# A Fourier transform and MLP kernel on one Trainium2 core: a fourth output buffer, a new place for the broadcast rows, and earlier transforms

## The chip, the cores and the metric

The kernel runs on one core of a Trainium2 chip. The metric is the device time in microseconds (us) of one execution; of several executions the median is given.

The names used below are those of the profile: PE is the engine of matrix multiplications, DVE the vector engine, ACT the scalar (activation) engine, POOL the GpSimd engine, SP the engine that here only issues transfers. Each engine runs its instructions in the order of the program and waits at an instruction whose inputs or buffers are not free.

## What is computed

The reference takes the real part of a Fourier transform over the last two axes of `x` (4 batches of 3008 rows by 256 columns) and sends each row through a two-layer MLP with the function g = h / (1 + exp(-h)) between the layers.

```python
X = np.fft.fft(x, axis=1)
X = np.fft.fft(X, axis=2)
x = X.real.reshape(B * S, D)      # 12032 rows of 256
h = x @ w_in                      # 256 x 2048, given as float64
g = h * (1.0 / (1.0 + np.exp(-h)))
out = g @ w_out                   # 2048 x 256, given as float64
```

## The kernel before

The kernel uses the symmetries of the transform, so that only 1506 of 3008 frequencies of each batch are carried; the result for a frequency and that for its mirror come out together (the two signs of the code).

**Chunks and steps.** The 4 x 1506 frequencies are cut into 13 chunks: four of 376 or 378 columns for the first batch and nine of 502 for the other three. For each chunk a loop runs over 16 steps f, one for each 128 columns of the hidden layer, so there are 208 steps; step (c, f) is step f of chunk c. In a step PE does `first`, six matmuls into a PSUM tile `pq` (lines 398 to 400), and then `second` for the step three before it (`LAG`), twelve matmuls into four accumulators `acc` (lines 456, 457, 463). Values are split into a high and a low part, hence three products for each. DVE adds the terms (lines 412, 416, 417; line 412 also reads `ub`, a row that was broadcast over all partitions), ACT applies the function and copies the high part (lines 428, 429), DVE makes the low part `gl` (line 439). After the last step of a chunk ACT copies the four accumulators into tiles `o` (line 471) and SP writes them out (line 472).

**The transform of the rows.** The inputs of a chunk come from 16 "classes" c, four to each batch. For each class the rows of x are loaded in two halves h into tiles `raw` (`load_x` by SP, then `add_x`, an accumulating transfer issued by POOL), folded by POOL with some copies by ACT (`fold_sums`, `fold_diffs`), combined by DVE into an operand `xf` (`operand`), copied as `xh` by ACT (line 298), and its low part `xl` made by POOL (line 305, three or five instructions). Then PE runs `transform` (line 330, 18 or 30 matmuls) into a `pq` tile, and `spread` takes it out: ACT copies the high part (line 370) and one row into a small tile `row` (line 373), a transfer broadcasts that row into `ub` (line 374), and DVE makes the low part (line 377). There are two buffers of `pq`, which `first` and `transform` take in turn, two of `raw`, and one each of `xf`, `xh` and `xl`.

**What sets the order.** There is no scheduler: every engine's order is that in which the program writes the instructions. Within a step it is `first`, `second`, the `transform` that falls due, `act` (DVE, ACT), `rest` of the step before (line 439), `spread`, then what the table `plan` has for the step (loads, adds, beginnings of folds), and a piece of the work that waits in two queues, one for DVE's operands and one for POOL's folds. `turns` holds the step in which a class is transformed, `begins` the step in which its operand is begun. Both tables are numbers written by hand.

**Buffers.** The tiles `o` and the tiles `row` share one tag with three buffers. The tag `half` has three buffers too; the conversion of the weights uses it in the time before and during chunk 0 (tiles `wf`).

Of the kernel before, what the change touches and what calls it, by code (L numbers as in the profile page):

```python
# [24 lines left out]
F32 = mybir.dt.float32  # L25
# [12 lines left out]
CH = 502  # L38
# [14 lines left out]
def fft_mlp(ctx, tc, x1, x2, w_in, w_out, te, to, t2, t2f, rot1, rot2, dft, eye, out):  # L53
# [6 lines left out]
    fold_p = ctx.enter_context(tc.tile_pool(name="fold", bufs=1))  # L60
# [89 lines left out]
    raw_x, folded, ready = {}, {}, set()  # L150
    every, lo, up = slice(0, 128), slice(0, 64), slice(64, 128)

    def load_x(k, i, ps=every):
        for h in range(2):
            t = raw_x[k, i, h] = raws.tile([128, 4, D], F32, tag="raw", name="raw")
            nc.sync.dma_start(out=t[ps], in_=(x1, x2)[k][i, ps, 0, h])

    def add_x(k, i, ps=every):

        for h in range(2):  # L160
            nc.gpsimd.dma_start(out=raw_x[k, i, h][ps], in_=(x1, x2)[k][i, ps, 1, h], accum_op=ALU.add)

    def fold_tile(name, k, i):
# [193 lines left out]
    def spread(c, po):  # L357

        b, k = divmod(c, 4)
        o, n = CLASS[k]  # L360
        o += b * NC
        parts = []
        for j, (at, m) in enumerate(zip(STARTS, CHUNKS)):
            lo, hi = max(o, at), min(o + n, at + m)
            if lo < hi:
                uvh, uvl, ub, _, _ = chunk(j)
                src, dst = slice(lo - o, hi - o), slice(lo - at, hi - at)
                parts.append((uvh[:, :, dst], uvl[:, :, dst], ub[:, dst], src))
        for uvh, _, _, src in parts:
            nc.scalar.activation(uvh, po[:, :, src], AF.Copy)  # L370
        for _, _, ub, src in parts:
            row = mp.tile([1, CH], F32, tag="o", name="row", bufs=3)[:, :src.stop - src.start]
            nc.scalar.activation(row, po[0:1, 1, src], AF.Copy)  # L373
            (nc.sync if c else nc.gpsimd).dma_start(
                out=ub, in_=row.unsqueeze(0).to_broadcast([1, 128, src.stop - src.start]))
        for uvh, uvl, _, src in parts:
            tt(uvl, po[:, :, src], uvh.bitcast(F32), op=ALU.subtract)  # L377
        if c == 0:

            for p, uv in enumerate(chunks[0][:2]):  # L380
                nc.scalar.activation(vneg[:, p, :n], uv[:, 1, :n].bitcast(F32), AF.Copy, scale=flip[:, :])
# [59 lines left out]
    def second(c, f):  # L441
        g = gs.pop((c, f))
        n, o = chunks[c][3:]
        if f == 0:
            accs[c] = [acc_p.tile([128, 512], F32, tag=f"acc{i}", name=f"acc{i}") for i in range(4)]

        if c or f >= FULL:
            gh, gl, _ = g

        def large(i):  # L450
            sg, es = i // 2, slice(i % 2 * 128, i % 2 * 128 + 128)
            po = accs[c][i][:, :n]
            if c == 0 and f < FULL:
                nc.tensor.matmul(po, wo_f32[f // 2][:, f % 2, es], g[:, sg, :n], start=f == 0, stop=False)  # L454
                return
            nc.tensor.matmul(po, wo[0][f // 2][:, f % 2, es], gh[:, sg, :n], start=f == 0, stop=False)  # L456
            nc.tensor.matmul(po, wo[1][f // 2][:, f % 2, es], gh[:, sg, :n], start=False, stop=False)  # L457

        def small(i):
            sg, es = i // 2, slice(i % 2 * 128, i % 2 * 128 + 128)  # L460
            if c == 0 and f < FULL:
                return
            nc.tensor.matmul(accs[c][i][:, :n], wo[0][f // 2][:, f % 2, es], gl[:, sg, :n], start=False, stop=f == NF - 1)  # L463

        if f == NF - 1:
            for i in range(4):
                large(i)
                small(i)
            for i, acc in enumerate(accs.pop(c)):
                t = mp.tile([128, CH], F32, tag="o", name="o", bufs=3)  # L470
                nc.scalar.activation(t[:, :n], acc[:, :n], AF.Copy)  # L471
                nc.sync.dma_start(out=out[i // 2, i % 2, :, o:o + n], in_=t[:, :n])
        else:
            for i in range(4):
                large(i)
            for i in range(4):
                small(i)
# [136 lines left out]
    def at(j, f, fn, *a):  # L614
        j, f = j + f // NF, f % NF
        plan.setdefault((j, f), []).append((fn, a))
# [1 line left out]
    def add(q, name, work):  # L618
        q.append((name, work))

    turns, begins = {}, {1: (0, 3), 2: (1, 9), 3: (2, 0), 4: (3, 2), 5: (3, 7), 6: (4, 0)}
    for c in range(1, 4):
        turns[c - 1, 12 + 2 * (c == 2)] = c
    for b in range(1, B):
        j, c = 3 * b + 1, 4 * b
        for k, when in enumerate(((j - 1, 0 if b > 1 else 7), (j - 1, 12 if b > 1 else 14), (j, 8), (j + 1, 4))):
            turns[when] = c + k
            begins.setdefault(c + k + 1, when)
        begins[c + 4], begins[c + 6] = (j + 1, 8), (j + 3, 3)
# [8 lines left out]
        at(j, f + 5 - (j < 3), add_x, k, i, *ps)  # L638
        at(j, f + 8 - (j < 3), add, pool_queue, (name, k, i), {"sm": fold_sums, "ri": fold_diffs}[name](k, i, *ps))

    at(0, 9, add, pool_queue, ("ri", 0, 0), fold_diffs(0, 0))
    fold("ri", 1, 0, 0, 13)
    fold("sm", 0, 1, 1, 9)
    fold("sm", 1, 0, 2, 5, up)
    fold("ri", 0, 1, 3, 1)
    for b in range(1, B - 1):
        j = 3 * b + 1
        fold("sm", 0, b + 1, j, 0)
# [156 lines left out]
```

## Time and profile before

| | us |
|---|---|
| median of 3 runs | 916.06 |
| lowest, highest | 915.75, 917.35 |
| the profiled execution | 916.99 |
| its span, first to last instruction | 915.2 |
| PE busy in the span | 881.5 |
| DVE, ACT, POOL busy | 718.9, 504.2, 173.2 |

Busy time of PE is modelled at the end of a matmul: in a stream of matmuls of 502 columns each is shown as 0.39 us long, but the next one starts 0.23 us after it. So a recorded idle time of PE is about 0.16 us shorter than the time that was lost. With 376 columns the pitch is 0.17 us. An undisturbed step lasts 18 pitches, 3.1 us for 376 columns and 4.1 us for 502.

The column PEclk of the windows is the share of full speed that TensorE's clock was granted.

### The profile page before, as it was taken

To read this page: it belongs to the slowest core of one execution; us is meant where nothing else is said; L and a number is where in the kernel's file an instruction comes from. 1 tells how busy PE (TensorE), PEld (TensorE's weight loads), DVE (VectorE), ACT (ScalarE), POOL (GpSimd) and SP (SyncE) were. 2 spreads that over 40 slices of the span, in tenths; PEclk is the share of its full clock that TensorE was granted. 3 is DMA by queue.
4 is the path that set the end of the run, shared out by engine and by line. 5 is a ranking of instruction groups with operands and counts; after the bars stand their busy time and mean duration, and the time that the engine had idled before them with its cause. 6 is when DMAs were issued, how large, how long until landed. Compare 5 with 4: busy or idle time off the path is not lost.

```text
span 915.2 us, 10977 instructions
## 1 busy us (share of the span) xinstructions
PE 881.5 (96%) x4118; PEld 751.8 (82%) x4118; DVE 718.9 (79%) x1023; ACT 504.2 (55%) x642; POOL 173.2 (19%) x211
## 2 busy tenths in 40 slices
PE   6899999899989999999998999999999999999997
PEld 4666899899988888887887888888788888888886
DVE  5887896879878786878877887787977877777874
ACT  3635674645566456466546555555655655545554
POOL 1115234210451240033403410023200110000000
PEclk9999999999999999999999999999999999999999
DMA  9790715304505241325225021322102120300101
GB/s 294 168 289 1 135 47 55 81 2 88 55 5 114 25 94 45 55 47 99 47 9 134 4 9 45 55 42 12 47 1 9 46 9 1 54 1 1 46 1 45
DMA packets 23205, 53.02 MB, mean 58 GB/s; under 512 B 3648, under 2 KB 12352, under 8 KB 22640
## 3 DMA queue, kind: packets, MB, share of 16 engines
q1 hardware_dynamic: 19280, 37.12, 19.7%
q0 software_dynamic: 3872, 15.20, 9.1%
q8 instruction: 32, 0.52, 0.2%
q14 instruction: 21, 0.17, 0.1%
HBM read 36.88 MB, written 12.34 MB: 54 GB/s over the span
## 4 chain that ended last, share of the span: by engine, by line
PE 85%; DVE 5%; DMA 4%; ACT 3%; issue 2%; POOL 1%; SPq 0%; ACTq 0%; DVEq 0%
PE acc L463 17%; PE acc L456 17%; PE acc L457 16%; PE pq L398 9%; PE pq L399 9%; PE pq L400 9%; PE pq L330 5%; PE acc L454 2%; DMA out_dram<-o 2%; DMA ub<-row 1%; DMA win<-in_w_in_dram 1%; PE pw L523 1%; DVE h L412 1%; PE pq L207 1%; DVE h L416 1%
## 5 line engine op out<-in xcount | busy, mean ns | idle before, releaser
L428 ACT ACTIVATE h<-h 128x1004 f32<-128x1004 f32 (+3 forms) x198 | 194.1, 980 | 299.3 <-DVE h L417 296.3
L456 PE MATMUL acc<-gh,woh 128*128 128x502 f32 (+2 forms) x784 | 296.3, 378 | 7.6 <-ACT o L471 7.5
L457 PE MATMUL acc<-gh,wol 128*128 128x502 f32 (+2 forms) x784 | 295.0, 376 | 0.0
L439 DVE TENSOR_TENSOR gl<-h,gh 128x1004 fp32r<-128x1004 f32 (+3 forms) x198 | 234.5, 1185 | 6.8 <-ACT gh L429 6.8
L412 DVE SCALAR_TENSOR_TENSOR h<-ub,a,pq 128x502 f32<-128x502 f32 (+2 forms) x206 | 143.5, 697 | 90.9 <-PE pq L400 80.7
L463 PE MATMUL acc<-gl,woh 128*128 128x502 f32 (+2 forms) x784 | 206.4, 377 | 0.0
L429 ACT ACTIVATE gh<-h 128x1004 fp32r<-128x1004 f32 (+3 forms) x198 | 194.3, 981 | 6.3
L456 PEld LDWEIGHTS acc<-gh,woh 128*128 128x128 f32 x784 | 149.1, 190 | 33.4 <-ACT o L471 11.1
L398 PE MATMUL pq<-uv,abh 128*128 128x502 f32 (+2 forms) x412 | 157.7, 383 | 8.8 <-DVE h L417 5.9
L457 PEld LDWEIGHTS acc<-gh,wol 128*128 128x128 f32 x784 | 148.5, 189 | 21.3
L463 PEld LDWEIGHTS acc<-gl,woh 128*128 128x128 f32 x784 | 146.1, 189 | 23.7
L399 PE MATMUL pq<-uv,abh 128*128 128x502 f32 (+2 forms) x412 | 154.6, 375 | 0.0
L400 PE MATMUL pq<-uv,abl 128*128 128x502 f32 (+2 forms) x412 | 154.5, 375 | 0.0
L417 DVE TENSOR_TENSOR h<-h,pq 128x502 f32<-128x502 f32 (+2 forms) x206 | 131.5, 639 | 7.1
L416 DVE TENSOR_TENSOR h<-h,pq 128x502 f32<-128x502 f32 (+2 forms) x206 | 131.4, 638 | 6.8
L305 POOL TENSOR_TENSOR xl<-xf,xh 128x256 fp32r<-128x256 f32 x53 | 50.8, 987 | 398.3 <-ACT xh L298 382.7
L398 PEld LDWEIGHTS pq<-uv,abh 128*128 128x128 f32 x412 | 77.9, 189 | 23.9 <-DVE h L417 9.1
L399 PEld LDWEIGHTS pq<-uv,abh 128*128 128x128 f32 x412 | 77.8, 189 | 12.4
L400 PEld LDWEIGHTS pq<-uv,abl 128*128 128x128 f32 x412 | 78.1, 189 | 11.9
L377 DVE TENSOR_TENSOR uv<-pq,uv 128x752 fp32r<-128x752 f32 (+4 forms) x22 | 15.5, 725 | 58.4 <-ACT row L373 58.4
L471 ACT ACTIVATE o<-acc 128x502 f32<-128x502 f32 (+2 forms) x52 | 28.1, 556 | 28.1 <-DMA out_dram<-o 16.3
L240 POOL TENSOR_TENSOR ri<-ri,raw 128x256 f32<-128x256 f32 x24 | 19.6, 816 | 89.2 <-ACT ri L237 88.5
(110 smaller groups left out, 518.5 us busy)
## 6 DMA issues: line engine op xcount, KB each, us to landing
raw<-in_x_dram SPq DMA_DIRECT2D x20, 512.0 KB, 8.8
raw<-in_x_dram POOLq DMA_DIRECT2D x20, 512.0 KB, 7.3
out_dram<-o SPq DMA_DIRECT2D x36, 251.0 KB, 2.1
win<-in_w_in_dram SPq DMA_DIRECT2D x8, 512.0 KB, 9.4
wo<-in_w_out_dram SPq DMA_DIRECT2D x8, 512.0 KB, 10.6
out_dram<-o SPq DMA_DIRECT2D x12, 188.0 KB, 2.3
ub<-row SPq DMA_DIRECT2D x8, 188.0 KB, 8.5
te<-in_te_dram POOLq DMA_DIRECT2D x1, 1128.0 KB, 11.8
```

Of the source, the lines that this page charges most:

```text
L398: nc.tensor.matmul(po, abh[:, i, fs], uvh[:, i, :n], start=True, stop=False)
L399: nc.tensor.matmul(po, abh[:, i, fs], uvl[:, i, :n], start=False, stop=False)
L400: nc.tensor.matmul(po, abl[:, i, fs], uvh[:, i, :n], start=False, stop=True)
L412: stt(p[:, :n], ub[:, :n], a128[f // 2][:, f % 2:f % 2 + 1], pq[:, 0, :n], op0=ALU.mult, op1=ALU.add)
L416: tt(h[:, 0, :n], p[:, :n], pq[:, 1, :n], op=ALU.add)
L417: tt(h[:, 1, :n], p[:, :n], pq[:, 1, :n], op=ALU.subtract)
L428: nc.scalar.activation(h[:, sg, :n], h[:, sg, :n], AF.Silu)
L429: nc.scalar.activation(gh[:, sg, :n], h[:, sg, :n], AF.Copy)
L439: tt(gl[:, sg, :n], g[:, sg, :n], gh[:, sg, :n].bitcast(F32), op=ALU.subtract)
L456: nc.tensor.matmul(po, wo[0][f // 2][:, f % 2, es], gh[:, sg, :n], start=f == 0, stop=False)
L457: nc.tensor.matmul(po, wo[1][f // 2][:, f % 2, es], gh[:, sg, :n], start=False, stop=False)
L463: nc.tensor.matmul(accs[c][i][:, :n], wo[0][f // 2][:, f % 2, es], gl[:, sg, :n], start=False, stop=f == NF - 1)
```

## The change

The diff does five things.

- The tag `o` holds four buffers instead of three, and no longer the rows.
- The rows of `spread` are taken from the tag `half`.
- `load_x` and `add_x` can be asked for one half alone. For class ri(1, 0) the two halves are loaded at steps (0, 11) and (0, 13) and added at (0, 15) and (1, 1); both were loaded at (0, 13) and added at (1, 1).
- Four transforms of the first five chunks stand earlier: class 2 at step (1, 12) instead of (1, 14), class 4 at (3, 3) instead of (3, 7), class 5 at (3, 11) instead of (3, 14); their operands and those of class 6 begin two to four steps earlier.
- The folds that feed them begin one to four steps earlier.

Everything after chunk 4 stands in the same order as before.

```diff
+    def load_x(k, i, ps=every, hs=range(2)):
+        for h in hs:
...
-            row = mp.tile([1, CH], F32, tag="o", name="row", bufs=3)[:, :src.stop - src.start]
+            row = fold_p.tile([1, 512], F32, tag="half", name="row", bufs=3)[:, :src.stop - src.start]
...
-                t = mp.tile([128, CH], F32, tag="o", name="o", bufs=3)
+                t = mp.tile([128, CH], F32, tag="o", name="o", bufs=4)
...
-    turns, begins = {}, {1: (0, 3), 2: (1, 9), 3: (2, 0), 4: (3, 2), 5: (3, 7), 6: (4, 0)}
+    turns, begins = {}, {1: (0, 3), 2: (1, 7), 3: (2, 0), 4: (2, 14), 5: (3, 4), 6: (3, 15)}
...
-        turns[c - 1, 12 + 2 * (c == 2)] = c
+        turns[c - 1, 12] = c
...
-        for k, when in enumerate(((j - 1, 0 if b > 1 else 7), (j - 1, 12 if b > 1 else 14), (j, 8), (j + 1, 4))):
+        for k, when in enumerate(((j - 1, 0 if b > 1 else 3), (j - 1, 12 if b > 1 else 11), (j, 8), (j + 1, 4))):
...
-    at(0, 9, add, pool_queue, ("ri", 0, 0), fold_diffs(0, 0))
-    fold("ri", 1, 0, 0, 13)
-    fold("sm", 0, 1, 1, 9)
-    fold("sm", 1, 0, 2, 5, up)
-    fold("ri", 0, 1, 3, 1)
+    at(0, 8, add, pool_queue, ("ri", 0, 0), fold_diffs(0, 0))
+    for h in range(2):
+        at(0, 11 + 2 * h, load_x, 1, 0, every, (h,))
+        at(0, 15 + 2 * h, add_x, 1, 0, every, (h,))
+    at(1, 2, add, pool_queue, ("ri", 1, 0), fold_diffs(1, 0))
+    fold("sm", 0, 1, 1, 8)
+    fold("sm", 1, 0, 2, 3, up)
+    fold("ri", 0, 1, 2, 14)
```

Three places show what this does to the order of an engine.

POOL in chunk 3, where the low parts of class 5 (line 305, five instructions) meet the fold of ri(0, 1) (lines 225 to 240, one half after the other):

```order
 L231 TENSOR_TENSOR raw<-raw 128x127
 L232 TENSOR_TENSOR raw<-raw 128x127
+L240 TENSOR_TENSOR ri<-ri,raw 128x256 x2
 L305 TENSOR_TENSOR xl<-xf,xh 128x256 x5
-L240 TENSOR_TENSOR ri<-ri,raw 128x256 x2
 L225 TENSOR_TENSOR raw<-raw 128x512
 L228 TENSOR_TENSOR raw<-raw 128x2x127
```

The end of the fold's first half moves ahead of the five low parts; its second half stays behind them.

ACT in chunk 3, from the copies of the fold's second half (lines 229, 236, 237) to the spread of class 5 (line 370), before the change:

```order
216 L229 ACTIVATE raw<-raw 128x4
217 L236 ACTIVATE raw<-raw,rot_sb_104 128x256
218 L237 ACTIVATE ri<-raw,rot_sb_104 128x256
219 L236 ACTIVATE raw<-raw,rot_sb_104 128x256
220 L237 ACTIVATE ri<-raw,rot_sb_104 128x256
221 L428 ACTIVATE h<-h 128x2x376
222 L429 ACTIVATE gh<-h 128x2x376
223 L370 ACTIVATE uv<-pq 128x2x126
```

and after it:

```order
208 L229 ACTIVATE raw<-raw 128x4
209 L236 ACTIVATE raw<-raw,rot_sb_104 128x256
210 L237 ACTIVATE ri<-raw,rot_sb_104 128x256
211 L236 ACTIVATE raw<-raw,rot_sb_104 128x256
212 L237 ACTIVATE ri<-raw,rot_sb_104 128x256
213 L428 ACTIVATE h<-h 128x2x376
214 L429 ACTIVATE gh<-h 128x2x376
215 L428 ACTIVATE h<-h 128x2x376
216 L429 ACTIVATE gh<-h 128x2x376
217 L370 ACTIVATE uv<-pq 128x2x126
```

The functions of two steps (lines 428, 429) now stand between the copies and the spread, where one stood.

SP in chunk 0, around the broadcast of class 1's row into `ub`:

```order
 L104 DMA wo<-in_w_out_dram 128x2x256 x5
+L156 DMA raw<-in_x_dram 128x1024
 L374 DMA ub<-row 128x1x378
-L156 DMA raw<-in_x_dram 128x1024 x2
+L156 DMA raw<-in_x_dram 128x1024
 L472 DMA out_dram<-o 128x376 x4
```

The first half of ri(1, 0) is loaded ahead of that broadcast and the second behind it.

## Rows read from the trace of the kernel before

**Rows 1.** Page, busy time: us, share of the span, instructions

```profile
PE 881.5 (96%) x4118; PEld 751.8 (82%) x4118; DVE 718.9 (79%) x1023; ACT 504.2 (55%) x642; POOL 173.2 (19%) x211
```

**Rows 2.** Waits of PE: line, what ended them, us in all, times, longest

```profile
PE acc L456 <- ACT o L471: 7.5, 6, 2.6
PE pq L398 <- DVE h L417: 5.9, 6, 2.4
PE pq L398 <- DVE uv L377: 2.9, 1, 2.9
```

**Rows 3.** Windows: stretch; PE, PEld, DVE, ACT, POOL busy (instructions); PEclk, DMA, GB/s

```profile
160.00:180.00 20.00, 16.68 (x87) 16.06 (x86) 17.35 (x29) 12.33 (x19) 3.84 (x5) 0.91 0.35 83
180.00:200.00 20.00, 20.00 (x118) 20.00 (x117) 17.74 (x28) 10.17 (x13) 6.57 (x6) 1.00 0.06 11
240.00:260.00 20.00, 19.70 (x114) 19.17 (x113) 17.56 (x32) 11.08 (x16) 7.58 (x8) 1.00 0.39 31
260.00:280.00 20.00, 17.07 (x98) 16.14 (x97) 12.88 (x22) 11.22 (x20) 7.90 (x10) 0.91 0.33 37
500.00:520.00 20.00, 19.05 (x77) 15.67 (x78) 14.56 (x21) 11.53 (x12) 5.12 (x6) 0.91 0.19 44
```

**Rows 4.** Timeline of PE, step (7, 3): start, length, line, [idle before <- releaser]

```profile
497.95 0.38 PE L457 MATMUL acc<-gh,wol 128*128 128x502 f32 x1
500.95 0.50 PE L456 MATMUL acc<-gh,woh 128*128 128x502 f32 x1 [2.61 <-ACT o L471]
```

**Rows 5.** Timeline of PE, step (9, 3)

```profile
642.32 0.50 PE L456 MATMUL acc<-gh,woh 128*128 128x502 f32 x1 [0.36 <-ACT o L471]
642.66 0.39 PE L457 MATMUL acc<-gh,wol 128*128 128x502 f32 x1
```

**Rows 6.** Timeline of the end: last matmul and last output copy

```profile
910.12 0.38 PE L463 MATMUL acc<-gl,woh 128*128 128x502 f32 x1
911.24 0.59 ACT L471 ACTIVATE o<-acc 128x502 f32<-128x502 f32 x1 [0.78 <-DMA out_dram<-o]
```

**Rows 7.** Timeline of SP and DVE around the start of chunk 2

```profile
152.47 0.48 SPq L374 DMA_DIRECT2D ub<-row  x1
161.10 0.61 DVE L412 SCALAR_TENSOR_TENSOR h<-ub,a,pq 128x376 f32<-128x376 f32 x1 [4.81 <-DMA ub<-row]
```

**Rows 8.** Timelines of ACT, POOL, DVE: from class 5's operand to its spread

```profile
254.83 1.26 ACT L298 ACTIVATE xh<-xf 128x1280 fp32r<-128x1280 f32 x1
256.17 4.70 POOL L305 TENSOR_TENSOR xl<-xf,xh 128x256 fp32r<-128x256 f32 x5 [11.80 <-ACT xh L298]
262.92 1.29 POOL L225 TENSOR_TENSOR raw<-raw 128x512 f32<-128x512 f32 x1
266.54 0.51 ACT L236 ACTIVATE raw<-raw,rot_sb 128x256 f32<-128x256 f32 x1 [2.09 <-POOL raw L232]
268.16 0.82 ACT L428 ACTIVATE h<-h 128x752 f32<-128x752 f32 x1
269.74 0.84 ACT L370 ACTIVATE uv<-pq 128x252 fp32r<-128x252 f32 x2
271.01 1.01 DVE L377 TENSOR_TENSOR uv<-pq,uv 128x252 fp32r<-128x252 f32 x2 [5.93 <-ACT row L373]
```

**Rows 9.** Timeline of POOL and ACT: low parts of class 3, fold of ri(0, 1)

```profile
173.21 2.17 POOL L305 TENSOR_TENSOR xl<-xf,xh 128x256 fp32r<-128x256 f32 x3 [15.62 <-PE pq L400]
240.53 1.29 POOL L225 TENSOR_TENSOR raw<-raw 128x512 f32<-128x512 f32 x1 [3.66 <-DMA raw<-in_x_dram]
251.16 0.19 ACT L229 ACTIVATE raw<-raw 128x4 f32<-128x4 f32 x1
```

**Rows 10.** Timeline of PE, ACT, DVE before chunk 0: class 0's row and the weights

```profile
31.56 1.89 PE L523 MATMUL pw<-wf,once 128*128 128x256 f32 x8
32.45 0.46 ACT L373 ACTIVATE row<-pq 1x376 f32<-1x376 f32 x1
34.04 0.93 DVE L377 TENSOR_TENSOR uv<-pq,uv 128x752 fp32r<-128x752 f32 x1
```

More of the change, by code (lines that the diff above doesn't have):

```diff
@@ L151, in fft_mlp, with add_x @@
     every, lo, up = slice(0, 128), slice(0, 64), slice(64, 128)
-    def load_x(k, i, ps=every):
-        for h in range(2):
+    def load_x(k, i, ps=every, hs=range(2)):
+        for h in hs:
             t = raw_x[k, i, h] = raws.tile([128, 4, D], F32, tag="raw", name="raw")
             nc.sync.dma_start(out=t[ps], in_=(x1, x2)[k][i, ps, 0, h])
-    def add_x(k, i, ps=every):
-        for h in range(2):
+    def add_x(k, i, ps=every, hs=range(2)):
+        for h in hs:
             nc.gpsimd.dma_start(out=raw_x[k, i, h][ps], in_=(x1, x2)[k][i, ps, 1, h], accum_op=ALU.add)
```

## The prediction

> **What bounds the kernel now.** The page comes first: PE is busy 96% of the span, DVE 79%, the others far less [rows 1]. So the end is set by PE, and what can be won is the time in which PE waits or runs at a low clock. The list of PE's waits is the second view: six waits for ACT's output copy, 7.5 us; six for DVE's sums, 5.9 us with one of 2.4; one for the low part of a spread, 2.9 us [rows 2]. The windows are the third: a stretch without a wait holds 118 matmuls of 376 columns, the stretch at 160 us only 87, and three stretches show a clock of 0.91 [rows 3]. In each of these three PE had just waited 2.4 to 2.9 us. Where the mean of 20 us is 0.91, part of it was granted at 1.2 instead of 2.4 GHz; that loses 0.09 x 20 = 1.8 us, rounded 1.7 to 1.9; I take **1.7 for each cut**.
>
> A recorded wait is too short, because the matmul before it is drawn 0.38 or 0.39 us long where the next could have begun after 0.23: 0.16 is added. The first matmul after a wait also holds the next one back, 0.34 instead of 0.23 us [rows 5], which adds 0.1. So a wait costs its recorded time and 0.26.
>
> **The change part by part.**
>
> *a. The output copies.* A chunk has four output tiles and three buffers, so the fourth copy waits until the first one's transfer has landed; the last copy of all shows this as idle time ended by a transfer [rows 6]. PE's next chunk needs the accumulator that this copy empties. Where a spread falls due shortly before, its rows hold buffers of the same tag. With four buffers of their own, each tile was last used a whole chunk (16 steps, 50 us or more) before, so this wait is gone whatever the transfers do. The six waits are 7.5 + 6 x 0.26 = 9.1 us. Not all of it goes: at step (9, 3) PE waits 0.36 us for the first copy [rows 5], which three buffers can't explain; there ACT has the copies of a fold to run first, and it still has. That leaves 0.36 + 0.26 = 0.6. **Gain 8.5 us.** If ACT is late at more of the six places, as little as 7.5.
>
> *b. The clock after the longest of them,* at (7, 3) [rows 3, 4], is not cut: **gain 1.7.**
>
> *c. The row of class 2.* Its broadcast is issued at 152.47 and the first sum of chunk 2 waits for it 4.8 us, until 161.10 [rows 7]. PE, which has two `pq` to fill, loses only 2.4 + 0.2 of that, and then 1.7 at the low clock [rows 2, 3]. The transform moves two steps, 6.2 us, forward. The row then lands 6.2 - 4.8 = 1.4 us before DVE wants it, and DVE could wait another 2.2 before PE does. **Gain 4.3.** The operand of class 2 begins two steps earlier as well, so the work from operand to transform keeps its five steps; the fold that feeds it moves two steps too.
>
> *d. DVE behind in chunk 3.* The stretch from 240 us holds 114 matmuls instead of 118 [rows 3]: 4 x 0.17 = 0.7 us, in which PE waits for sums. There the low part of class 4's spread and the three pieces of class 5's operand stand in three steps in a row. Now the spread stands at (3, 3) and the pieces at (3, 4) to (3, 6), one step more for the same work. I let 0.2 stay. **Gain 0.5**, from 0 to 0.7.
>
> *e. The spread of class 5.* This is the term that I expect to disappoint. At 272 us PE waits 2.9 + 0.2 = 3.1 us for the low part of this spread, and 1.7 at the low clock follow [rows 2, 3]: 4.8. The transform moves from (3, 14) to (3, 11), four steps ahead of its chunk. But PE needs the spread for a second reason: `first` two steps after a transform takes the same one of the two `pq` buffers. Before, that was `first` of (4, 0), the chunk's own start; now it is `first` of (3, 13). What makes the spread late is a chain [rows 8]: class 5's high part ends on ACT at 256.1; then POOL runs five low parts (4.7), two instructions of the fold (2.0, between 260.87 and 262.92) and the start of the fold's second half (until 266.5); ACT, which stands at the copies of that half, waits for it, copies (1.6), runs the functions of one step (1.6), then the spread, and DVE ends it at 272.0. That is 15.9 us. In the new order the two fold instructions stand ahead of the low parts (-2.0), and the functions of two steps instead of one stand between copies and spread (+1.6): 15.5. PE's way is as long as before, six steps and the transform: from (3, 7) to (3, 13) where it was from (3, 10) to (4, 0). It is shorter by the 0.5 of d, which lay on it; and the operand's pieces meet a DVE that has one step less behind it, so that the chain starts some 0.3 earlier. The wait is then 3.1 - 0.4 + 0.5 - 0.3 = 2.9, call it 2.8, and the clock is cut as after the other three. 2.8 + 1.7 = 4.5 stays. **Gain 0.3**, from -0.5 (every POOL instruction at its slowest) to 4.8.
>
> *f. The end.* The last matmul is drawn to 910.50, the last copy starts at 911.24 [rows 6]. With its own buffer it starts at 910.55. **Gain 0.7.**
>
> *Edits that I cost at nothing.* Rows in `half`: the row of class 0 now takes the buffer of a weight tile that PE reads until 33.45, so it is written 1.0 us later than 32.45. Its cover is DVE, which comes to the spread only at 34.04 [rows 10]; without that cover it would be 1.0. The half loads: the first now stands ahead of class 1's broadcast on SP, which waits if the load's buffer isn't free; chunk 1 begins without a wait, so there is nothing to gain, and the bound above is one more wait like that of c, 4.3. The adds that stand earlier on POOL come behind the same low parts as before. Class 6's high part now stands ahead of chunk 3's output copies on ACT, 0.8 us, where PE has no wait.
>
> **Sum.** 8.5 + 1.7 + 4.3 + 0.5 + 0.3 + 0.7 = 16.0 us. The profiled execution took 916.99, so 901.0 by it. The median of the runs is 0.9 lower, 916.06; by that **900.1 us**.
>
> **The rivals.**
>
> *1. The spread of class 5 isn't waited for at all* (the change does what it says): 4.5 more, 895.6. It needs the chain to be 2.8 us shorter than 15.5. For it: four steps are much more than PE's six matmuls. Against: the order of ACT and POOL leaves the chain as it is.
>
> *2. The chain is shorter because POOL is.* Three low parts of class 3 took 2.17 us, 0.72 each, and five of class 5 took 4.70, 0.94 each [rows 8, 9]. At 0.72 the five take 3.6 and the wait is 1.7, recorded as 1.5. Whether the clock is cut after so short a wait, no row shows. Without a cut 4.5 becomes 1.7: 897.3; with it 899.0. I keep the slow price, since it is the one of this place. The Trainium skill, GPSIMD Engine Reference, section 8 (Key points), says that POOL shares its interfaces to SBUF with DVE and is held up by DVE instructions with two inputs in SBUF. By that rule the slow price holds wherever the low part of `gl` (line 439) runs beside, as it does here in each step, and the sum is 900.1; by the fast price it would be 897.3.
>
> The Trainium skill's first page, Trainium Kernel Development and Optimization, section Best Practices, says that bubbles that recur can mean that SBUF or PSUM ran out. By that rule the wait of e is one of two PSUM buffers, which no earlier step adds to; it speaks against this part of the change and for 900.1 instead of 895.6.
>
> *3. The fourth buffer changes nothing,* since something else holds the copies: a, b and f stay, 10.9 us, 911.0. Against it: the one copy that has no other work around it waits for a transfer [rows 6].
>
> *4. A small new wait in chunks 0 to 2,* with a cut: 2.6 + 1.7 = 4.3, so 904.4.
>
> *5. Slower than before.* Place: the fold of ri(0, 1). POOL's first instruction of it waited 3.66 us for the add, and ended at 241.8; ACT read it at 251.16 [rows 9]. All of it moves with the transform, so 9.3 us of slack remain. A later add holds ACT at its copies, ACT holds both spreads of chunk 3, and PE stops. Each us beyond 9.3 costs one; to lose the 16.0 and 1.8 more the add must come 27 us later, against its load and POOL. Nothing in the rows asks for that.
>
> **How the numbers follow.** Forecast 0.57; rival 1: 0.17; rival 2: 0.14; rival 3: 0.03; rival 4: 0.06; rival 5: 0.02; no difference for another reason 0.01. The forecast's own bounds are about 898.9 to 901.6 (a down to 7.5, e to -0.5, d at 0 or 0.7, small terms). Rivals 1 and 2 lie below, so the range goes down to 895.0; rival 4 is mostly left out: 895.0 to 903.5. A measurement of this kernel tells 0.2%, 1.8 us, from no change. Faster by more: 0.96; within: 0.02; slower: 0.02.
>
> **What would show it.** Right: no wait of ACT for an output transfer; matmul counts of 118 in the windows of chunk 2; one wait of PE of 2.5 to 3 us at a `first` in chunk 3, ended by line 377, two steps after class 5's transform, with one stretch at a clock of about 0.9; a last copy that follows the last matmul at once. Wrong: no wait there (rival 1) or one under 2 us (rival 2); a transform that waits for its low part; a first sum of chunk 1 or 2 that waits for its row; output copies that still wait.

## The result, and the profile of the changed kernel

The changed kernel takes **902.08 us**, the median of four executions (901.38 to 905.69), where the kernel before took 916.7 beside it; the ratio is **0.9845, with an interval of 0.9813 to 0.9877**. The profiled execution took 901.38 us: 15.6 us less than the profiled one of before, where the sum of the prediction was 16.0.

| us | before | after |
|---|---|---|
| profiled execution | 916.99 | 901.38 |
| its span | 915.2 | 899.6 |
| PE busy | 881.5 | 876.2 |
| start of step (1, 0) | 99.66 | 99.68 |
| end of the last matmul | 910.50 | 895.54 |
| span behind the last matmul | 4.7 | 4.1 |

The two profiles are level until the start of step (1, 0), so everything lies behind it. The page's row of busy time answers [rows 1]:

```profile
PE 876.2 (97%) x4118; PEld 748.5 (83%) x4118; DVE 718.6 (80%) x1023; ACT 504.1 (56%) x642; POOL 175.8 (20%) x211
```

PE has the same 4118 matmuls and is busy 5.3 us less, 5.0 of it after the start of (1, 0). The stretches at 1.2 GHz (called cuts of the clock here) cost 4.8 us before and 1.4 after, which makes 3.4. The other 1.6 fit six waits fewer, each of which the profile counts 0.26 us too short. The list of PE's waits (engine, what waited, what ended it: us in all, times, longest) answers [rows 2]:

```profile
PE pq L398 <- DVE h L417: 3.3, 5, 1.7
PE pq L398 <- DVE uv L377: 2.5, 1, 2.5
PE acc L456 <- ACT o L471: 0.4, 1, 0.4
```

Six waits for the output copies have become one of 0.4 that the list shows; the wait of 2.4 for DVE's sums is gone (the five that are left lie in chunk 0 and, with 0.3, in chunk 3); the wait for the spread of class 5 is still there, 2.5 instead of 2.9. The wait from which term a started was ACT's own, for the transfers of earlier output tiles. In the kernel before, it stands in the list as

```profile
ACT o L471 <- DMA out_dram<-o: 16.3, 11, 4.7
```

and the list of the changed kernel has no such line. The windows (columns as in [rows 3]) show the same by place:

```profile
160.00:180.00 20.00, 20.00 (x118) 20.00 (x117) 17.38 (x28) 13.16 (x18) 11.22 (x11) 1.00 0.39 92
225.00:245.00 20.00, 19.70 (x113) 19.00 (x112) 19.13 (x33) 12.70 (x18) 8.81 (x11) 1.00 0.20 8
250.00:270.00 20.00, 17.52 (x92) 16.95 (x91) 14.93 (x25) 10.97 (x17) 0.74 (x1) 0.91 0.41 64
500.00:520.00 20.00, 20.00 (x93) 17.06 (x93) 15.03 (x20) 9.46 (x14) 9.44 (x9) 1.00 0.14 6
```

The start of chunk 2 and the stretch at 500 us are full and at 2.4 GHz. The one stretch at 0.91 that is left is that of class 5's spread. The stretch at 225 us lacks five of its 118 matmuls, as that at 240 us lacked four in [rows 3]: DVE is still late once in chunk 3.

The row of class 2 is now issued 7.8 us earlier than in [rows 7] (6.2 for the two steps and 1.6 for the wait at (1, 3) that is gone), and the first sum of chunk 2 (line 412, 128x376) waits for PE alone:

```profile
144.64 0.47 SPq L374 DMA_DIRECT2D ub<-row  x1
153.85 0.61 DVE L412 SCALAR_TENSOR_TENSOR h<-ub,a,pq 128x376 f32<-128x376 f32 x1 [0.22 <-PE pq L400]
```

At the end [rows 6] the last matmul starts at 895.16, and the four output copies run in one piece behind the matmuls that release them, without a transfer between:

```profile
895.16 0.38 PE L463 MATMUL acc<-gl,woh 128*128 128x502 f32 x1
893.55 2.62 ACT L471 ACTIVATE o<-acc 128x502 f32<-128x502 f32 x4 [4.96 <-PE acc L463]
```

What each step lost follows from the first matmuls (line 398) of two steps that follow each other: their distance, less that of an undisturbed step. By it the 15.6 us divide as follows.

| term | place | lost before | lost after | gain | predicted |
|---|---|---|---|---|---|
| a | (1, 3), (2, 3), (6, 3), (7, 3), (9, 3) | 9.6 | 1.1 | 8.4 | 8.5 |
| b | cut behind (7, 3) | 1.57 | 0 | 1.6 | 1.7 |
| c | (2, 1), (2, 2) | 4.17 | 0 | 4.2 | 4.3 |
| d | (3, 10) to (3, 12), after: (3, 8) to (3, 10) | 0.73 | 0.70 | 0.0 | 0.5 |
| e | (3, 15), (4, 0), after: (3, 12), (3, 13) | 4.70 | 4.02 | 0.7 | 0.3 |
| f | behind the last matmul | 4.70 | 4.06 | 0.6 | 0.7 |

The sum is right to 0.5 us, and a, b, c and f are right one by one; d brought nothing, and e stayed for the reason given. (By its diff the change moves three transforms, those of classes 2, 4 and 5, and begins class 6's operand one step earlier; the description ahead of the prediction says four transforms and two to four steps.) The experiments ask whether the terms are what the table takes them for, and what d and e hang on.

### The profile page after: what moved, and what is told of

Read it like the earlier page. It is cut to its first block, busy times and chain, and to the rows that moved or that the text cites. A ratio compares the mean times of both kernels' runs of the same rounds, so it can differ in the third digit from the quotient of the medians.

```text
span 899.6 us, 10975 instructions
## 1 busy us (share of the span) xinstructions
PE 876.2 (97%) x4118; PEld 748.5 (83%) x4118; DVE 718.6 (80%) x1023; ACT 504.1 (56%) x642; POOL 175.8 (20%) x211
## 4 chain that ended last, share of the span: by engine, by line
PE 87%; DVE 6%; DMA 2%; ACT 2%; issue 2%; POOL 1%; SPq 0%; ACTq 0%
PE acc L456 18%; PE acc L463 18%; PE acc L457 18%; PE pq L398 9%; PE pq L399 9%; PE pq L400 9%; PE pq L330 5%; DMA wo<-in_w_out_dram 1%; DMA win<-in_w_in_dram 1%; PE acc L454 1%; PE pq L207 1%; DVE h L412 1%; DVE h L416 1%; POOL xl L305 1%; DVE h L417 1%
## 5 line engine op out<-in xcount | busy, mean ns | idle before, releaser
L305 POOL TENSOR_TENSOR xl<-xf,xh 128x256 fp32r<-128x256 f32 x53 | 54.4, 1056 | 379.7 <-ACT xh L298 366.1
L377 DVE TENSOR_TENSOR uv<-pq,uv 128x752 fp32r<-128x752 f32 (+4 forms) x22 | 15.5, 725 | 53.4 <-ACT row L373 53.4
```

## The experiments

The table gives the length from the first matmul of (1, 0) to the end of the last one beside the times, since chunk 0, which the change hardly touches, differs from profile to profile by up to 3.7 us (see the last section). Ratios are to the kernel before, run beside; its medians were 916.7, 917.8 and 919.2 us in the three sets with several executions, so ratios of different sets differ by up to 0.3% for that alone.

| kernel | median us | ratio (interval) | profiled: (1, 0) to last matmul |
|---|---|---|---|
| before | | 1 | 810.8 |
| changed | 902.08 | 0.9845 (0.9813 to 0.9877) | 795.9 |
| buf_only | 905.43 | 0.9847 (0.9820 to 0.9874) | 799.2 |
| buf4_shared | 905.23, one execution | | 799.1 |
| tables_only | 911.58 | 0.9914 (0.9887 to 0.9942) | 803.7 |
| c2_undo | 905.66, one execution | | 798.6 |
| halves_undo | 903.07 | 0.9846 (0.9826 to 0.9866) | 794.6 |
| c5_late | 900.4 | 0.9815 (0.9794 to 0.9836) | 792.5 |
| fold_after | 898.44 | 0.9793 (0.9771 to 0.9815) | 791.0 |
| pool_beside | 898.38, one execution | | 791.2 |
| act_beside | 896.75, one execution | | 791.0 |
| best | 897.96 | 0.979 (0.977 to 0.981) | 791.5 |
| best2 | 898.62 | 0.977 (0.9738 to 0.9802) | 789.9 |

### The buffers alone, and whether the rows' place matters

buf_only is the kernel before with two lines changed; buf4_shared changes only the number.

```diff
-            row = mp.tile([1, CH], F32, tag="o", name="row", bufs=3)[:, :src.stop - src.start]
+            row = fold_p.tile([1, 512], F32, tag="half", name="row", bufs=3)[:, :src.stop - src.start]
...
-                t = mp.tile([128, CH], F32, tag="o", name="o", bufs=3)
+                t = mp.tile([128, CH], F32, tag="o", name="o", bufs=4)
```

> The kernel before with two lines changed: four buffers for the output tiles and the broadcast rows in the small tag; transforms, folds and loads stand where they stood. Theory (the changes add up: terms a, b and f of the prediction are the buffers' alone): no wait of ACT for an output transfer, no wait of PE for the output copy beyond 0.4 us, the cut of the clock at 501 us gone, the last copy right behind the last matmul; 8.3 + 1.7 + 0.65 = 10.6 us less than the kernel before, ratio 0.988 to 0.989. The waits of 2.4 us at (2, 1) and 2.9 us at (4, 0) stay. Rival (the earlier tables took a part of those waits, the buffers only the rest): 5 to 8 us less, and some step (c, 3) still waits more than 0.4 us.

> The kernel before with the shared tag of output tiles and rows at four buffers, the rows still in it. Theory of the prediction (the count is what matters where no row stands between; a row takes one of the four): the waits at (6, 3), (9, 3) gone as with the rows apart, and those where a spread stands shortly before the output copies, (1, 3), (2, 3), (7, 3), smaller or gone, since a row's buffer is free as soon as its small broadcast has landed: 9 to 11 us less. Rival (the rows' own place does most of it): a wait of 1 us or more for the output copy stays at (2, 3) or (7, 3), and less than 7 us is gained.

PE's waits of buf_only:

```profile
PE pq L398 <- DVE h L417: 5.4, 4, 2.3
PE pq L398 <- DVE uv L377: 2.9, 1, 2.9
PE acc L456 <- ACT o L471: 0.4, 1, 0.4
```

The waits for the output copies are those of the changed kernel, the other two those of before. The steps (c, 3) and (7, 4) give 10.0 us and the end 0.7, 10.7 in all. The length from (1, 0) is shorter by 11.6 and not by 10.0, because in this execution the wait of 2.9 us was not followed by a cut of the clock. So its ratio of 0.9847 is lower than the expected 0.988 to 0.989 by something that is not the buffers'. buf4_shared has the same steps within 0.1 us: for these two terms it is the number of buffers that counts, and the rows' own place adds nothing as long as the transforms stand where they stood. Terms a, b and f are confirmed, and rival 3 falls.

### The tables alone

The changed kernel with three buffers shared with the rows (the diff above, backwards).

> The changed kernel with three output buffers shared with the rows, as before; transforms, folds and half loads keep their new places. Theory (terms c, d, e alone): the wait at (2, 1) is gone with its cut, 4.2 us, and of the one for class 5's spread 0.7 us is gone; about 5 us less than the kernel before, ratio 0.994 to 0.995; the waits at (1, 3), (2, 3), (6, 3), (7, 3), (9, 3) are those of the kernel before. Rival (the tables and the buffers need each other, since the rows of earlier transforms hold output buffers earlier): waits at (2, 3) or (4, 3) that differ by more than 0.5 us from before, and a ratio off by 0.002 or more.

```profile
PE acc L456 <- ACT o L471: 6.7, 7, 2.7
PE pq L398 <- DVE uv L377: 2.5, 1, 2.5
```

The wait at (2, 1) and its cut are gone, 4.2 us. But the waits for the output copies are not those of before: (1, 3) and (2, 3) lose 1.8 us less, and (3, 3) and (4, 3), where before had no such wait, lose 1.4. So the rival was right in this: with three shared buffers the new tables change which output copy waits, and a part of the waits of a went with the tables while others came. Which transform, row or load made which of them was not tried. From (1, 0) on the kernel is 7.1 us shorter than before; 1.4 to 1.7 of that is again a cut that did not follow the wait for class 5's spread. The two halves of the change give 10.0 and some 5.6 us without such luck, together 15.6, and the change gave 15.0 before its end: nearly the sum.

### The row of class 2

```diff
-        turns[c - 1, 12] = c
+        turns[c - 1, 12 + 2 * (c == 2)] = c
```

and class 2's operand begun at (1, 9) instead of (1, 7).

> The changed kernel with class 2 transformed at (1, 14) again, its operand begun at (1, 9). Theory (term c: the broadcast of the row, 8.5 us long, is what the first sum of chunk 2 waits for): the wait of DVE for ub at the start of chunk 2 comes back, about 4.8 us, and PE loses 2.4 + 0.2 at (2, 1), with up to 1.7 more if the clock is cut after it; 2.6 to 4.3 us longer from the start of (1, 0) to the last matmul. Rival (the row was late because of what else was moved, the earlier folds or the rows' new buffers): the wait is under 3 us and PE loses less than 1 us.

```profile
152.41 0.47 SPq L374 DMA_DIRECT2D ub<-row  x1
161.02 0.60 DVE L412 SCALAR_TENSOR_TENSOR h<-ub,a,pq 128x376 f32<-128x376 f32 x1 [4.80 <-DMA ub<-row]
```

The rows are those of [rows 7] to 0.1 us, and (2, 1) and (2, 2) lose 4.1 us again. From (1, 0) on the kernel is only 2.7 us longer than the changed one, since its wait for class 5's spread (2.47 us) was not followed by a cut. The theory holds: 8.5 us of broadcast that started too late, and nothing else that was moved.

### The half loads

```diff
-    for h in range(2):
-        at(0, 11 + 2 * h, load_x, 1, 0, every, (h,))
-        at(0, 15 + 2 * h, add_x, 1, 0, every, (h,))
+    at(0, 13, load_x, 1, 0)
+    at(1, 1, add_x, 1, 0)
```

> The changed kernel with both halves of ri(1, 0) loaded at (0, 13) and added at (1, 1), as before; the fold's begin and all transforms stay early. Theory (the half loads are not needed): the adds land some 4 to 9 us later, still by about 108 to 111 us, just when ACT comes to the first copy of the fold; no wait of PE over 0.5 us in chunk 1 or at class 2's transform, 902 us. Rival (they carry class 2's earlier transform): ACT is held at the copies in chunk 1, PE waits 2 us or more there or at transform 2, 904 to 906 us.

All steps of chunk 1 stay at 3.1 us, and the transform of class 2 does not wait. The half loads are worth nothing here, as the prediction costed them. This kernel's length is 1.2 us under the changed one's for another reason, below.

### Why class 5's spread is still waited for

Two kernels take the chain of [rows 8] apart. c5_late puts the transform back to (3, 14), so that it is no longer four steps ahead of its chunk:

```diff
-        for k, when in enumerate(((j - 1, 0 if b > 1 else 3), (j - 1, 12 if b > 1 else 11), (j, 8), (j + 1, 4))):
+        for k, when in enumerate(((j - 1, 0 if b > 1 else 3), (j - 1, 12 if b > 1 else 14), (j, 8), (j + 1, 4))):
```

with the operand from (3, 7). The whole fold of ri(0, 1) then stands ahead of class 5's low parts on POOL.

> The changed kernel with class 5's transform put back to (3, 14) and its operand's begin to (3, 7); the fold of ri(0, 1) stays early, so all of it now stands ahead of the five low parts on POOL and of the spread on ACT. Theory (chain): PE waits for the spread of class 5 because ACT is held at the copies of the fold's second half, not because the transform is late. Then PE's wait of 2.48 us in chunk 3 and the low clock after it are gone although the transform is only two steps ahead of its chunk: no wait over 0.5 us at (4, 0), 4.0 us less, and some of the 0.7 us at (3, 8) too, since the operand's pieces no longer follow class 4's spread: about 897.5 us. Rival (lead): a transform needs four steps ahead of its chunk; then first of (4, 0) waits about 3 us with a clock cut, as before the change, and the time is 902 to 903 us.

fold_after leaves the transform at (3, 11) and puts the whole fold behind the low parts instead:

```diff
-    fold("ri", 0, 1, 2, 14)
+    at(2, 14, load_x, 0, 1)
+    at(3, 2, add_x, 0, 1)
+    at(3, 10, add, pool_queue, ("ri", 0, 1), fold_diffs(0, 1))
```

with class 6's operand from (4, 0).

> The changed kernel with the fold of ri(0, 1) begun on POOL at (3, 10) instead of (3, 5), so that it stands behind class 5's five low parts and its copies behind the spread on ACT (class 6's operand begins at (4, 0) again). Transform 5 stays at (3, 11). Theory (chain): the wait of PE at (3, 13) and its low clock go, about 4.0 us less, 898 us; the 0.7 us at (3, 8) stay. Rival (DVE and PE alone make the spread late): nothing changes, 902 us with a wait of 2 to 3 us at (3, 13).

First the changed kernel's own chain, from the timelines of ACT, POOL, DVE and PE (start, length, engine, line, [idle before <- releaser]), which answers [rows 8]:

```profile
238.41 1.25 ACT L298 ACTIVATE xh<-xf 128x1280 fp32r<-128x1280 f32 x1
239.75 4.93 POOL L305 TENSOR_TENSOR xl<-xf,xh 128x256 fp32r<-128x256 f32 x5 [2.51 <-ACT xh L298]
244.64 1.29 POOL L225 TENSOR_TENSOR raw<-raw 128x512 f32<-128x512 f32 x1
248.26 0.51 ACT L236 ACTIVATE raw<-raw,rot_sb 128x256 f32<-128x256 f32 x1 [2.09 <-POOL raw L232]
249.88 0.82 ACT L428 ACTIVATE h<-h 128x752 f32<-128x752 f32 x1
251.47 0.82 ACT L428 ACTIVATE h<-h 128x752 f32<-128x752 f32 x1
253.05 0.84 ACT L370 ACTIVATE uv<-pq 128x252 fp32r<-128x252 f32 x2
254.33 1.01 DVE L377 TENSOR_TENSOR uv<-pq,uv 128x252 fp32r<-128x252 f32 x2 [1.79 <-ACT row L373]
255.48 0.65 PE L398 MATMUL pq<-uv,abh 128*128 128x376 f32 x1 [2.48 <-DVE uv L377]
```

The low parts, the start of the fold's second half (POOL until 248.2), ACT held at its copies, the functions of two steps, then the spread: from 239.66 to 255.34, 15.7 us, where 15.5 was predicted. And in fold_after, ACT and DVE in the same place:

```profile
249.36 0.84 ACT L370 ACTIVATE uv<-pq 128x252 fp32r<-128x252 f32 x2
250.50 0.49 ACT L236 ACTIVATE raw<-raw,rot_sb 128x256 f32<-128x256 f32 x1
250.63 1.01 DVE L377 TENSOR_TENSOR uv<-pq,uv 128x252 fp32r<-128x252 f32 x2 [2.06 <-ACT row L373]
```

The spread now comes right behind the functions of one step, and the fold's copies after it. The list of PE's waits of this kernel has no line for L377 any more, and no step of chunk 3 is over its length. In c5_late that line is gone too, with (3, 14), (3, 15) and (4, 0) undisturbed, though the transform has one whole step of lead instead of four; it loses 0.7 us anew at (4, 3), where ACT's output copies come late:

```profile
275.64 0.83 ACT L298 ACTIVATE xh<-xf 128x768 fp32r<-128x768 f32 x1
276.38 1.59 ACT L471 ACTIVATE o<-acc 128x376 f32<-128x376 f32 x4
```

Class 6's high part (line 298) stands ahead of them. The prediction had costed this order at nothing, and in the changed kernel, which has it too, it costs nothing; but there, after the wait for class 5's spread, PE begins (4, 3) at 276.49, 0.14 us before the copies, and in c5_late at 274.92, 1.46 us before them. fold_after has the high part behind the copies and loses nothing there. So c5_late gains 3.4 us from (1, 0) on, where 4.0 and a part of d's loss were expected, and its median of 900.4 us misses the expected 897.5; chunk 0, with two cuts of the clock in its profile, adds to that.

The lead was not what the wait for the spread hung on; the fold between the low parts on POOL and the spread on ACT was. Against the expectation d's loss went too in fold_after, which is the next question.

### Why d brought nothing

fold_after loses nothing in these steps, with the spread of class 4 and the operand of class 5 in the same steps as in the changed kernel. So with one step more the crowding that the prediction blamed no longer costs anything; it takes the fold beside it. On DVE the changed kernel shows, in the steps in which the fold ran:

```profile
224.70 1.20 DVE L439 TENSOR_TENSOR gl<-h,gh 128x752 fp32r<-128x752 f32 x1
225.82 0.95 DVE L269 TENSOR_TENSOR sm<-sm 128x512 f32<-128x512 f32 x1
226.78 0.85 DVE L270 TENSOR_TENSOR sm<-sm 64x512 f32<-64x512 f32 x1
236.69 1.34 DVE L439 TENSOR_TENSOR gl<-h,gh 128x752 fp32r<-128x752 f32 x1
238.14 0.61 DVE L412 SCALAR_TENSOR_TENSOR h<-ub,a,pq 128x376 f32<-128x376 f32 x1
```

and fold_after for the same five instructions:

```profile
224.74 0.94 DVE L439 TENSOR_TENSOR gl<-h,gh 128x752 fp32r<-128x752 f32 x1
225.59 0.68 DVE L269 TENSOR_TENSOR sm<-sm 128x512 f32<-128x512 f32 x1
226.29 0.69 DVE L270 TENSOR_TENSOR sm<-sm 64x512 f32<-64x512 f32 x1
236.03 0.94 DVE L439 TENSOR_TENSOR gl<-h,gh 128x752 fp32r<-128x752 f32 x1
237.07 0.61 DVE L412 SCALAR_TENSOR_TENSOR h<-ub,a,pq 128x376 f32<-128x376 f32 x1
```

0.26 + 0.27 + 0.16 + 0.40 = 1.09 us longer, and the last row starts 1.07 later: that is all of DVE's delay up to there. POOL's fold lay beside them until 227.1 and again from 235.7; two of its rows:

```profile
226.18 0.91 POOL L232 TENSOR_TENSOR raw<-raw 128x127 f32<-128x127 f32 x1
235.71 1.53 POOL L240 TENSOR_TENSOR ri<-ri,raw 128x256 f32<-128x256 f32 x2 [8.62 <-ACT ri L237]
```

c5_late, which loses 0.7 us at (3, 10) to (3, 12), has no spread beside class 5's operand but the fold: there line 439 takes 1.51 us and line 269 takes 1.22. In the kernel before, lines 269 and 270 took 0.73 and 0.85, so only 0.2 us of its loss can have come this way; there the prediction's reading, spread and operand on top of each other, fits the rows, though no run tested it alone.

The rival is the fold's copies on ACT. Both were tested in fold_after, which has neither at this place: pool_beside adds work that nobody needs on POOL, act_beside on ACT.

```diff
+    def beside(c, f):
+        t, gh = fold_p.tile([128, 512], F32, tag="half", name="spare", bufs=3), gs[c, f][0].bitcast(F32)
+        for _ in range(3):
+            nc.gpsimd.tensor_tensor(t[:, :256], gh[:, 0, :256], gh[:, 1, :256], op=ALU.subtract)
+
+    for f in range(4, 8):
+        at(3, f, beside, 3, f)
```

> The changed kernel with the fold of ri(0, 1) begun at (3, 10), which has no loss at (3, 8) to (3, 10), plus work that is not needed: in each of the steps (3, 4) to (3, 7) POOL makes three differences of 128x256 of the step's gh into a spare tile that nobody reads. ACT gets no copies here. Theory (the 0.7 us that the changed kernel loses at (3, 8) to (3, 10) come from DVE instructions that last longer beside POOL: lines 269, 270 took 0.95 and 0.85 us beside the fold, 0.68 and 0.69 without it; line 439 took 1.34 beside line 240, 0.94 without): 12 instructions of about 0.9 us; the changed kernel's 5.6 us of fold beside DVE put DVE back by 1.1 us, so these 10.8 put it back by about 2 us, and PE loses 1 to 2 us in (3, 7) to (3, 11). Rival (the fold's five copies on ACT put the function, and so DVE, back): nothing is lost, the steps stay at 3.1 us.

```diff
+    def beside(c, f):
+        t, gh = fold_p.tile([128, 512], F32, tag="half", name="spare", bufs=3), gs[c, f][0].bitcast(F32)
+        for i in range(4):
+            nc.scalar.activation(t[:, :256], gh[:, i % 2, :256], AF.Copy)
+
+    at(3, 6, beside, 3, 6)
```

> The counterpart of the POOL run: the changed kernel with the fold of ri(0, 1) begun at (3, 10), plus four copies of 128x256 on ACT that nobody reads, behind the functions of step (3, 6), where the changed kernel has the four copies of the fold (lines 236, 237). POOL has nothing more to do. Theory (the 0.7 us at (3, 8) to (3, 10) come from DVE instructions that last longer beside POOL): lines 439 before and behind the copies stay at 0.94 us and PE loses nothing, steps of 3.1 us. Rival (the copies on ACT put the next function and so DVE back): line 428 of step (3, 7) starts late, and PE loses 0.3 to 0.7 us at (3, 8) to (3, 10).

In act_beside the four copies run, the next function starts in time, and line 439 keeps its 0.94 us:

```profile
234.37 1.77 ACT L652 ACTIVATE spare<-gh 128x256 f32<-128x256 f32 x4
236.31 0.84 ACT L428 ACTIVATE h<-h 128x752 f32<-128x752 f32 x1 [0.18 <-DVE h L417]
236.20 0.94 DVE L439 TENSOR_TENSOR gl<-h,gh 128x752 fp32r<-128x752 f32 x1
```

Every step of chunk 3 stays undisturbed; the rival falls. In pool_beside line 439 gets longer each time POOL works beside it, most here:

```profile
239.79 2.66 POOL L652 TENSOR_TENSOR spare<-gh 128x256 f32<-128x256 f32 x3 [1.73 <-ACT gh L429]
240.65 1.30 DVE L439 TENSOR_TENSOR gl<-h,gh 128x752 fp32r<-128x752 f32 x1
```

Over the four steps it is 0.08 + 0.13 + 0.08 + 0.36 = 0.65 us, and PE loses 0.13 at (3, 8) and (3, 9). The direction is the theory's, the size is not: 2 us and 1 to 2 us were expected. An average price for a microsecond of POOL was the wrong measure. Lines 412, 416 and 417, one input of which is in PSUM, kept 0.60 and 0.55 us throughout, whatever POOL did; what is lengthened are instructions whose inputs are both in SBUF, while POOL works beside them (by 0.08 us where they overlap for 0.23, by 0.36 in the rows above, where POOL works beside all of it). DVE behind by 0.65 us cost PE 0.13; behind by 1.07, in the changed kernel, it cost 0.52 at (3, 8): about 0.5 us of slack stood between in both. The other 0.18 of d's loss, at (3, 9) and (3, 10), comes with a third long instance of line 439, 1.46 us beside class 5's low parts on POOL. So POOL's work as the cause is shown by the two added loads; that it makes up the whole 0.7 us rests on the sums of these rows, as pool_beside brought back only 0.13.

The Trainium skill, SBUF — State Buffer, section "Who interferes with whom", says that a DVE instruction with two SBUF inputs contends with a GpSimd instruction that reads SBUF, and that one with at most one such input, outside DVE's two-port modes, does not. The trace agrees in both halves: line 439 takes 0.94 us alone and 1.20, 1.34 and 1.46 us beside POOL, and line 412 does not change.

### The two later folds, and the best order

At (6, 3) and (9, 3) the changed kernel still loses 0.46 and 0.68 us. ACT and PE show why, at (9, 3): four copies of a fold (lines 236 and 237, the first of them here) run ahead of the output copies, until 628.14.

```profile
626.55 0.49 ACT L236 ACTIVATE raw<-raw,rot_sb 128x256 f32<-128x256 f32 x1
...
628.14 2.00 ACT L471 ACTIVATE o<-acc 128x502 f32<-128x502 f32 x4
628.76 0.49 PE L456 MATMUL acc<-gh,woh 128*128 128x502 f32 x1 [0.36 <-ACT o L471]
```

best is c5_late, best2 is fold_after, each with the folds of ri(0, 2) and ri(0, 3) one step later:

```diff
-        fold("ri", 0, b + 1, j + 1, 6)
+        fold("ri", 0, b + 1, j + 1, 7)
```

> c5_late, and the folds of ri(0, 2) and ri(0, 3) one step later, so that ACT's four output copies at (6, 2) and (9, 2) stand ahead of the four copies of the fold's second half instead of behind them. Theory: the 0.46 us of (6, 3) and the 0.68 of (9, 3) that remain are ACT's and go, 1.1 us less than c5_late: about 896.3 us. Rival (the output copies wait for PE, not for ACT's other work): the same time as c5_late.

> The changed kernel with the fold of ri(0, 1) begun on POOL at step (3, 10), behind class 5's low parts, class 6's operand from (4, 0), and the folds of ri(0, 2) and ri(0, 3) one step later. Theory (the fold ahead of the low parts makes the wait at (3, 13); the copies of the later folds ahead of ACT's output copies make the 0.46 and 0.68 us at (6, 3) and (9, 3)): no step of chunks 1 to 12 over its undisturbed length by more than 0.1 us; 1.1 us less than with the first edit alone, 6 us less than the changed kernel, ratio about 0.978. Rival (the two edits disturb each other or the later folds come too late for their operands): a wait of a transform or of a fold's operand at (6, 12) or (9, 12), 1 us or more.

```profile
625.35 2.01 ACT L471 ACTIVATE o<-acc 128x502 f32<-128x502 f32 x4
630.53 0.49 ACT L236 ACTIVATE raw<-raw,rot_sb 128x256 f32<-128x256 f32 x1
```

That is ACT in best2: the output copies first, the fold's after the next function. In both kernels (6, 3) and (9, 3) are back at 4.1 us, 1.1 us gained. best keeps c5_late's two losses at (3, 11) and (4, 3), and its median of 897.96 us is above the expected 896.3; best2 has no step of chunks 1 to 12 over its undisturbed length by more than 0.1 us, and its list of PE's waits ends in chunk 0. From (1, 0) on it takes 6.0 us less than the changed kernel, about the sum of d, e and the 1.1. With a ratio of 0.977 to the kernel before (0.9738 to 0.9802) it beats both kernels; from best and fold_after, whose intervals overlap with its own, the times alone don't tell it.

## Why the prediction was right, point by point

**The bound.** The forecast of 900.1 us rested on PE's waits and the cuts of its clock, and the gain came from these alone. The profiled execution was met to 0.4 us (901.0 by the sum, 901.38). The median is 2.0 us higher than forecast: 0.9 had been taken off for the median of before, and in the run beside it before itself had 916.7 instead of 916.06. By the ratio the kernel of 916.06 us comes to 901.9. Both lie in the range of 895.0 to 903.5, but above the forecast's own bounds of 898.9 to 901.6. Those bounds don't follow from what is named with them: a down to 7.5, e at -0.5 and d at 0 together make 2.3 us, up to 902.4. And there was luck in the 0.4 us: neither of the two profiles has a cut in chunk 0, where other profiles start (1, 0) up to 3.5 us later, and the cut behind the wait for class 5's spread came, which it did in two of seven profiles; without it the execution would have been 1.4 us shorter.

**a, b and f** were right in mechanism and size: 8.4, 1.6 and 0.6 us for 8.5, 1.7 and 0.7. buf_only shows that they are the buffers'. The reservation at (9, 3), that copies of a fold stand ahead, was right; it holds at (6, 3) too, 0.46 us, which the bound of 7.5 allowed for.

**c** was right: 4.2 for 4.3, and c2_undo brings it back.

**d** failed. The step that failed is "one step more for the same work": the work was not the same length. The fold that moved with the transforms came to lie beside these very steps on POOL, and lengthened DVE's instructions by 1.09 us before (3, 9); PE lost 0.70 us where 0.2 had been left. The prediction had cited the contention of the two engines for POOL's side, in rival 2, and not asked what it does to DVE.

**e** stayed, as predicted, by the chain that was predicted: 15.7 us for 15.5, and the five low parts at the slow price, 4.93 us for 4.70. Rivals 1 and 2 fall. The wait cost 2.64 us in place of 2.8. The two errors hang together: PE's way to this wait contains d, so the 0.5 that d did not bring makes the 2.9 of the sum 0.5 shorter, 2.4, and the longer chain adds 0.2. d and e together gained 0.7, for 0.8 predicted.

**The rule on recurring bubbles**, cited from the Trainium skill's Trainium Kernel Development and Optimization, Best Practices, for this wait, was read as pointing at the two `pq` buffers. It spoke for 900.1 against 895.6, which came out; but the rule is about bubbles that recur, and this wait comes once in the trace. fold_after agrees with it only in part: with the same two buffers the wait is gone once the fold is out of the chain.

**The price of a cut, 1.7,** was right where a cut came (1.4 to 1.7) and wrong as a certainty. The last section has this.

**Rivals 4 and 5** did not show: no new wait in chunks 0 to 2, and the fold of ri(0, 1) was not late.

## What to carry to other kernels

A transfer or a transform that is begun earlier helps only if the engines that it passes through have nothing new ahead of it; so follow the whole chain of engines from operand to use, and move the bystanders (here a fold) before moving the thing that is late. When work on POOL is moved, look at which DVE instructions with both inputs in SBUF it will lie beside: they get longer though no wait is recorded. Buffers shared by two kinds of tiles can couple the place of one to the timing of the other (in tables_only waits for output copies moved by 1.4 to 1.8 us when only transforms, folds and loads did; that it was the rows was not shown). One more buffer was worth more here than all the reordering, 10.7 us against some 5.6, and the rows' new place and the half loads were worth nothing.

## What the runs showed of the hardware that was not expected

**A wait is not always followed by a cut of the clock.** The thirteen profiles hold 35 waits of PE between 2.2 and 3 us in the time after 20 us; 20 of them are followed by a stretch at 1.2 GHz and the others are not, with nothing in their length to tell them apart. In c2_undo a cut followed a wait of 1.90 us. The wait for class 5's spread is 2.48 us in the changed kernel and 2.46 us in halves_undo, after the same matmuls. Here is the first matmul behind it and the window in halves_undo:

```profile
257.44 0.41 PE L398 MATMUL pq<-uv,abh 128*128 128x376 f32 x1 [2.46 <-DVE uv L377]
250.00:270.00 20.00, 17.55 (x106) 17.02 (x106) 14.30 (x25) 12.65 (x20) 1.65 (x3) 1.00 0.41 64
```

Granted clock 1.00 and 106 matmuls, where the changed kernel had 0.91 and 92, and 0.65 us for that first matmul. That cut cost 1.4 us, and halves_undo, which loses 0.2 more at (3, 8) to (3, 10), is 1.2 us shorter. In buf_only and buf4_shared waits of 2.9 us went uncut, whereas the wait at (2, 1) was cut in all four kernels that have it. Of seven waits for class 5's spread two were cut. So a cut should have entered e with a chance and not with its full 1.7 us.

**Chunk 0 makes much of the scatter between profiles.** (1, 0) starts at 99.5 to 103.2 us in the thirteen profiles, at 99.7 in that of the changed kernel and at 103.2 in that of best2. A part of that is PE's first wait, which ends between 7.2 and 9.8 us (7.86 and 9.81 in these two). The rest goes with cuts: waits of 2.5 us at about 27 us and of 1.7 to 2.7 at about 65 to 70 us were cut in some profiles and not in others. Less the first wait, (1, 0) starts at 91.8 to 92.3 us in the four profiles without a cut in chunk 0 and at 93.4 to 94.8 in the four with two. The changed kernel's four executions took 901.38, 902.05, 902.1 and 905.69 us at granted clocks of 0.998, 0.996, 0.996 and 0.992. What decides whether a given wait is cut stays open.
